# A fused Fourier and two-layer kernel: the second w_out chunk converted in halves, stage A of the second batch entry begun three ticks earlier

## The chip, the cores and the metric

The kernel runs on one core of one Trainium2 chip. The metric is the device time of one execution in microseconds (us). The engines are named as the profile names them: PE (TensorE, matmuls), DVE (VectorE), ACT (ScalarE), POOL (GpSimd) and SP (SyncE, which issues most transfers). Each engine works through its own list of instructions in order and waits on semaphores for the others.

## The reference

```python
def _attn_ref(x) -> np.ndarray:            # x: (2, 3008, 256)
    X = np.fft.fft(x, axis=1)
    X = np.fft.fft(X, axis=2)
    return X.real.astype(np.float32)

def _moe_ref(x, w_in, w_out) -> np.ndarray:     # 6016 tokens, 256 -> 2048 -> 256
    h = x @ w_in
    alpha = 1.0
    g = np.where(h > 0.0, h, alpha * (np.exp(np.minimum(h, 0.0)) - 1.0))
    return (g @ w_out).astype(np.float32)

def _moe2_ref(x, w_in, w_out, alpha) -> np.ndarray:
    h = x @ w_in
    g = np.maximum(h, 0.0) + alpha * np.minimum(h, 0.0)
    return (g @ w_out).astype(np.float32)

def reference(**kwargs):
    ...
    x = attn_out.reshape(B * S, D)
    x = _moe_ref(x=x, **moe_kwargs)
    return _moe2_ref(x=x, **moe2_kwargs)
```

## The kernel before

The real part of the two-dimensional Fourier transform is taken in stages. Stage A is a transform of length 47, four chunks for each of the two batch entries, each chunk in two halves; a half is two PSUM tiles on PE (`stage_a`, L182) that ACT copies to `uc` (L184). When a chunk is whole, SP stores it to DRAM in three pieces (`store_u`) and later loads it back in another order (`load_v`). Stage B (L280, L281) is a transform of length 64; its result is kept as two parts, `hi` by ACT (L290) and `lo`, the remainder, by DVE (L365). The transform along the 256 features is multiplied into the first `w_in`, chunk by chunk (`w_fold`, L376).

All matrix products of the two layers are made of three passes over such pairs (`hi` with `hi`, `lo` with `hi`, `hi` with `lo`). Weights arrive as 64-bit words and are converted first: one ACT instruction (`conv_y`, L333) and three DVE steps (`conv_s`: step 0 at L351, step 1 at L353, step 2 at L355). A split (`w_split`, `hi_lo`) then makes `hi` on ACT (L430) and `lo` on POOL (L431).

The first layer runs in ticks. Tick t takes one block of tokens and 128 of the 2048 hidden columns. Ticks 0 to 7 take block 0 with columns 0 to 7 (in units of 128), ticks 8 to 15 block 1 with the same columns, and so on; four columns make a weight chunk. A tick holds:

- hooks that were put at `pre`
- gemm1(t): six matmuls into two PSUM tiles (L472)
- DVE: `pt` (L605, which reads `zb`) and two `ht` (L609)
- ACT: `hi` of tick t-2 (L584); then the hooks at `mid`; then relu (L625) and exp (L631) of tick t
- POOL: `lo` of tick t-2 (L590); DVE: the combine of tick t-1 (`et`, L577)
- hooks at `end`
- gemm2(t-3): twelve matmuls (L488). Its first matmul needs the `hi` part of the `w_out` half of its columns, its second the `lo` part. In tick 4 it is gemm2(1), in tick 7 gemm2(4), the first to read chunk 1 of `w_out`.

In tick 10, where gemm2(7) ends a group, DVE and ACT also copy the sums out (`xs`, L508, L506) ahead of the combine.

PSUM tiles for gemm1, stage A, stage B, delta and fold come from two pairs of banks, `mm` and `ee`, taken in turn by a counter: whoever adds or moves a tile changes the bank of all later ones.

The order is fixed by tables of tick numbers. `CONV1` has for each weight chunk the tick of the ACT instruction, the ticks of the three DVE steps (at `end`) and the ticks of the two splits; `STAGE_A1` has for each chunk of the second batch entry the tick and place of its halves. `FOLD` puts the fold of `w_in` chunk 2 at the start of tick 11. Delta (L230) is a small product at the start of tick 4, whose result ACT copies to `dt` (L233); stage B of block 1 stands at the start of tick 5.

Of the kernel before, what the change touches and what calls it, by code (L numbers as in the profile page):

```python
# [43 lines left out]
E_PSUM = 42  # L44


CONV1 = [
    (('o', 1, 1), 3, (4, 5, 6), (6, 7)),
    (('i', 1, 2), 7, (7, 8, 9), ()),
    (('i', 1, 3), 10, (10, 12, 13), ()),  # L50
    (('o', 1, 2), 14, (14, 15, 16), (17, 18)),
    (('o', 1, 3), 18, (18, 20, 21), (21, 22)),
]

STAGE_A1 = [
    (0, (7, 'pre'), (8, 'pre')), (1, (9, 'pre'), (11, 'pre')), (2, (12, 'pre'), (14, 'pre')), (3, (16, 'pre'), (17, 'pre')),
]
LOAD_X = {3: 9}
FOLD = {2: (11, 'pre', 0), 3: (15, 'pre', 0)}
# [40 lines left out]
def tile_fft_moe_elu_moe_prelu(  # L100
# [664 lines left out]
    def at(t, fn, *a, where="pre"):  # L765
        hooks[where].setdefault(t, []).append(lambda: fn(*a))
# [4 lines left out]
    def at_conv(t, ts, kind, layer, c, i=None):  # L771

        at(t, conv_y, kind, layer, c, i, where="mid")
        for step in range(3):
            at(ts[step], conv_s, kind, layer, c, i, step, where="end")

    def at_split(t, kind, layer, c, i):
        at(t, w_split, kind, layer, c, i, where="end")
# [7 lines left out]
    with tc.manual_schedule():  # L786
# [27 lines left out]
        }  # L814
        for what, *args in START:
            start[what](*args)
        at_conv(1, (1, 3, 3), "o", 1, 0, 1)
        at_split(3, "o", 1, 0, 1)
        for key, t, ts, splits in CONV1:
            at_conv(t, ts, *key)  # L820
            for i, t_split in enumerate(splits):
# [159 lines left out]
```

## Time and profile before

| what | value |
|---|---|
| device time, median of 3 runs | 962.52 us |
| lowest and highest | 962.43 and 964.06 us |
| device time of the profiled execution | 963.83 us |
| its span, first to last instruction | 961.6 us |
| mean granted TensorE clock | 0.998 |
| busy: PE, DVE, ACT, POOL | 947.0, 715.8, 654.4, 622.7 us |

The profile is of one execution, which took 963.83 us; 2.2 us of that lie outside its span. All places in the text are us from the start of that span. A busy PE says that matmuls were under way, not that the engine was at its peak.

### The profile page before, as it was taken

Reading aid. Unit: us, or ns where it says so; the run is one execution under the profiler, and the core shown is the slowest. Engines: PE = TensorE matmul, PEld = TensorE weight load, DVE = VectorE, ACT = ScalarE, POOL = GpSimd, SP = SyncE. Lnnn points to the kernel's source line nnn. Section 1 sums busy time; section 2 is a strip of 40 time slices with the busy share of each in tenths; the row PEclk is TensorE's granted clock in tenths of the full one; section 3 lists DMA queues with packets and bytes.
Section 4 is the critical chain, followed back from the end, with each engine's and each line's share of the span. In section 5 each row is a group of like instructions: output and inputs, shape, how many; then the busy total and the mean of one; then the engine's idle time right before and its main releaser. Section 6 shows DMA issues by size and latency. Waiting matters only on the chain.

```text
span 961.6 us, 12199 instructions
## 1 busy us (share of the span) xinstructions
PE 947.0 (98%) x4206; PEld 769.3 (80%) x4206; DVE 715.8 (74%) x1012; ACT 654.4 (68%) x914; POOL 622.7 (65%) x495
## 2 busy tenths in 40 slices
PE   8889999999999999999999999999999999999998
PEld 3666778789888878888888888889988888888886
DVE  2896899988999999887777666565657557566564
ACT  5677777766888888888766665565665556565553
POOL 1264577764968779987878855656565664664543
PEclk9999999999999999999999999999999999999999
DMA  8973322201222311121140110020010011001001
GB/s 325 321 228 79 96 77 89 99 25 65 78 75 81 136 44 34 45 88 44 44 154 1 39 45 0 1 88 1 1 56 28 0 45 44 1 1 45 0 1 44
DMA packets 27189, 64.10 MB, mean 67 GB/s; under 512 B 3124, under 2 KB 11572, under 8 KB 25080
## 3 DMA queue, kind: packets, MB, share of 16 engines
q1 hardware_dynamic: 25696, 62.09, 19.3%
q10 hardware_dynamic: 1176, 1.07, 0.3%
q8 instruction: 33, 0.54, 0.2%
q0 software_dynamic: 256, 0.17, 0.1%
q14 instruction: 28, 0.23, 0.1%
HBM read 41.53 MB, written 21.79 MB: 66 GB/s over the span
## 4 chain that ended last, share of the span: by engine, by line
PE 88%; DVE 5%; DMA 3%; ACT 1%; issue 1%; SPq 0%; POOL 0%; ACTq 0%; DVEq 0%
PE acc L488 50%; PE eet L667 13%; PE mmt L667 10%; PE mmt L472 9%; PE eet L472 2%; DMA w<-w_in 1%; DVE et L577 1%; DVE ht L609 1%; DVE pt L605 1%; PE mmt L182 1%; DMA nd<-dt 1%; PE eet L376 1%; PE mmt L281 1%; DMA xc<-x 1%; PE mmt L280 1%
## 5 line engine op out<-in xcount | busy, mean ns | idle before, releaser
L488 PE MATMUL acc<-hi,wo 128*128 128x512 f32 (+1 forms) x1536 | 430.5, 387 | 4.2 <-ACT wo L430 1.5
L693 POOL TENSOR_TENSOR lo<-et,hi 128x512 fp32r<-128x512 f32 (+1 forms) x190 | 237.6, 1281 | 181.0 <-ACT hi L687 181.0
L590 POOL TENSOR_TENSOR lo<-et,hi 128x512 fp32r<-128x512 f32 (+1 forms) x192 | 272.1, 1440 | 107.2 <-ACT hi L584 61.1
L488 PEld LDWEIGHTS acc<-hi,wo 128*128 128x128 f32 x1536 | 288.7, 188 | 61.1 <-ACT wo L430 2.0
L488 PE MATMUL acc<-lo,wo 128*128 128x512 f32 (+1 forms) x768 | 258.3, 387 | 1.3 <-POOL lo L590 1.1
L687 ACT ACTIVATE hi<-et 128x1024 fp32r<-128x1024 f32 (+1 forms) x96 | 100.3, 1045 | 132.5 <-PE acc L488 70.2
L488 PEld LDWEIGHTS acc<-lo,wo 128*128 128x128 f32 x768 | 144.1, 188 | 30.6 <-POOL lo L590 3.4
L625 ACT ACTIVATE et<-ht 128x1024 f32<-128x1024 f32 (+2 forms) x97 | 100.3, 1034 | 68.4 <-DVE ht L609 67.2
L719 DVE TENSOR_TENSOR v<-mmt,p 128x512 f32<-128x512 f32 (+1 forms) x48 | 32.7, 681 | 143.0 <-ACT p L714 143.0
L472 PE MATMUL mmt<-zt,wi 128*128 128x512 f32 (+1 forms) x444 | 116.5, 394 | 1.4 <-DVE ht L609 0.8
L584 ACT ACTIVATE hi<-et 128x1024 fp32r<-128x1024 f32 (+2 forms) x97 | 99.3, 1024 | 5.4 <-DVE et L577 3.9
L609 DVE TENSOR_TENSOR ht<-pt,mmt 128x512 f32<-128x512 f32 (+1 forms) x150 | 95.0, 674 | 8.4 <-PE acc L488 0.5
L472 PEld LDWEIGHTS mmt<-zt,wi 128*128 128x128 f32 x444 | 82.5, 188 | 23.1 <-DVE ht L609 3.4
L744 ACT ACTIVATE et<-mmt 128x512 f32<-128x512 f32 (+1 forms) x96 | 55.8, 590 | 28.8 <-PE mmt L667 14.7
L605 DVE SCALAR_TENSOR_TENSOR pt<-zb,an_sb,mmt 128x512 f32<-128x512 f32 (+1 forms) x73 | 53.4, 731 | 24.7 <-PE mmt L472 24.6
L577 DVE SCALAR_TENSOR_TENSOR et<-et,ht 128x1024 f32<-128x1024 f32 (+2 forms) x44 | 67.3, 1530 | 1.3 <-POOL lo L590 1.1
L574 DVE SCALAR_TENSOR_TENSOR et<-eet,ht 128x512 f32<-128x512 f32 (+1 forms) x106 | 67.1, 674 | 0.0
L747 DVE SCALAR_TENSOR_TENSOR et<-et,oma_sb,eet 128x512 f32<-128x512 f32 (+1 forms) x96 | 66.1, 730 | 0.0
L747 DVE SCALAR_TENSOR_TENSOR et<-et,oma_sb,mmt 128x512 f32<-128x512 f32 (+1 forms) x96 | 66.0, 728 | 0.0
L636 ACT ACTIVATE eet<-et 128x512 f32<-128x512 f32 (+1 forms) x106 | 58.9, 588 | 3.7 <-DVE et L574 2.1
L667 PE MATMUL eet<-xo,wi 128*128 128x512 f32 (+1 forms) x216 | 59.8, 385 | 0.0
L667 PE MATMUL mmt<-xo,wi 128*128 128x512 f32 (+1 forms) x216 | 59.8, 385 | 0.0
(123 smaller groups left out, 1241.6 us busy)
## 6 DMA issues: line engine op xcount, KB each, us to landing
w<-w_in SPq DMA_DIRECT2D x8, 1024.0 KB, 13.5
w<-w_out SPq DMA_DIRECT2D x7, 1024.0 KB, 8.9
ud<-uc SPq DMA_DIRECT2D x20, 256.0 KB, 4.1
vt<-ud SPq DMA_DIRECT2D x5, 1024.0 KB, 4.8
xd<-xs SPq DMA_DIRECT2D x10, 512.0 KB, 3.5
xs<-xd SPq DMA_DIRECT2D x5, 1024.0 KB, 4.8
out_t<-ot SPq DMA_DIRECT2D x16, 256.0 KB, 2.1
xc<-x SPq DMA_DIRECT2D x5, 768.0 KB
```

Of the source, the lines that this page charges most:

```text
L472: mm(out=p[:, 0:n], lhsT=lhsT, rhs=rhs, start=(i == 0), stop=(i == len(ops) - 1))
L488: mm(out=accs[L, bl][d][t][:, 0:n], lhsT=w[:, a, o, d * 128:(d + 1) * 128], rhs=(hi, lo)[b][:, t, 0:n], start=(f == first and i == 0), sto ...
L574: stt(out=s["e"][:, i, :], in0=s["x"][i], scalar=-1.0, in1=s["h"][:, i, :], op0=ALU.add, op1=ALU.max)
L577: stt(out=s["e"][:, i], in0=s["e"][:, i], scalar=-1.0, in1=s["h"][:, i], op0=ALU.add, op1=ALU.max)
L584: act(out=s["hi"][:, i, 0:s["n"]], in_=s["e"][:, i], func=ACTF.Copy)
L590: nc.gpsimd.tensor_tensor(out=s["lo"][:, i, 0:n], in0=s["e"][:, i, :], in1=s["hi"][:, i, 0:n].bitcast(F32), op=ALU.subtract)
L609: tt(out=ht[:, i, 0:n], in0=pt[:, 0:n], in1=p[1], op=op)
L625: act(out=s["e"][:, i], in_=s["h"][:, i], func=ACTF.Relu, scale=-1.0)
L667: mm(out=bank[:, 0:n], lhsT=w[:, a], rhs=x2[b][:, 0:n], start=(first and m == 0), stop=(last and m == 2), skip_group_check=True)
L687: act(out=s["hi"][f][:, :, 0:n], in_=s["g"][f], func=ACTF.Copy)
L693: eng.tensor_tensor(out=s["lo"][f][:, t, 0:n], in0=s["g"][f][:, t], in1=s["hi"][f][:, t, 0:n].bitcast(F32), op=ALU.subtract)
L747: stt(out=o, in0=o, scalar=oma_sb[:, 2 * j + f:2 * j + f + 1], in1=h, op0=ALU.mult, op1=ALU.add)
```

## The change

The list `HALVES` converts the two halves of chunk 1 of the first `w_out` one after the other, each with instructions of half the size: the first half's steps at the ends of ticks 4, 5 and 5, split in tick 6; the second's at the ends of ticks 6, 7 and 7, split in tick 8. Before, the whole chunk's steps stood in ticks 4, 5 and 6 and the splits in ticks 6 and 7. The last step and the split of the second half of chunk 0 move from tick 3 to tick 4. The conversion of `w_in` chunk 2 moves from ticks 7, 7, 8 and 9 to ticks 8, 8, 9 and 10. In stage A of the second batch entry, the first four halves move from ticks 7, 8, 9 and 11 to ticks 4 (at `mid`, behind gemm1), 6, 8 and 9.

```diff
+HALVES = [
+    (('o', 1, 0), 1, 1, (1, 3, 4), 4),
+    (('o', 1, 1), 0, 3, (4, 5, 5), 6),
+    (('o', 1, 1), 1, 5, (6, 7, 7), 8),
+]
 CONV1 = [
-    (('o', 1, 1), 3, (4, 5, 6), (6, 7)),
-    (('i', 1, 2), 7, (7, 8, 9), ()),
+    (('i', 1, 2), 8, (8, 9, 10), ()),
     (('i', 1, 3), 10, (10, 12, 13), ()),
...
 STAGE_A1 = [
-    (0, (7, 'pre'), (8, 'pre')), (1, (9, 'pre'), (11, 'pre')), (2, (12, 'pre'), (14, 'pre')), (3, (16, 'pre'), (17, 'pre')),
+    (0, (4, 'mid'), (6, 'pre')), (1, (8, 'pre'), (9, 'pre')), (2, (12, 'pre'), (14, 'pre')), (3, (16, 'pre'), (17, 'pre')),
 ]
...
-        at_conv(1, (1, 3, 3), "o", 1, 0, 1)
-        at_split(3, "o", 1, 0, 1)
+        for key, i, t, ts, t_split in HALVES:
+            at_conv(t, ts, *key, i)
+            at_split(t_split, *key, i)
```

PE in tick 4, before: delta, gemm1(4), then gemm2(1), whose last matmul is followed by stage B. (`acc` are the sums of gemm2, `r_sb` and `f_sb` the constants of stage B with delta and of stage A.)

```order
L230 MATMUL mmt<-r_sb,vt 8x64
L231 MATMUL mmt<-r_sb,vt 8x64
L472 MATMUL eet<-zt,wi_233 128x512 x6
L488 MATMUL acc_378<-hi,wo_290 128x512 x2
...
L488 MATMUL acc_381<-lo,wo_290 128x512
L280 MATMUL mmt<-r_sb,vt 128x2x64
```

The same place on PE after the change, where all lines of code are four further down.

```order
L234 MATMUL mmt<-r_sb,vt 8x64
L235 MATMUL mmt<-r_sb,vt 8x64
L476 MATMUL eet<-zt,wi_233 128x512 x6
L186 MATMUL mmt<-xc,f_sb 96x512 x2
L492 MATMUL acc_378<-hi,wo_290 128x512 x2
...
L492 MATMUL acc_381<-lo,wo_290 128x512
L284 MATMUL eet<-r_sb,vt 128x2x64
```

Two tiles of stage A stand between gemm1(4) and gemm2(1), in the `mm` banks, one of which delta has just written; stage B moves to the `ee` banks.

ACT from the middle of tick 3, before (`w_408` is chunk 1 of `w_out`, `wo_290` the split chunk 0):

```order
L333 ACTIVATE w_408<-w_252 128x1024
L625 ACTIVATE et<-ht 128x1024
L631 ACTIVATE et<-et 128x1024
L430 ACTIVATE wo_290<-w_270 128x512
L233 ACTIVATE dt<-mmt 8x64
L234 DMA nd_88<-dt 8x64
L584 ACTIVATE hi<-et 128x1024
L625 ACTIVATE et<-ht 128x1024
```

And after:

```order
L337 ACTIVATE w_408<-w_252 128x512
L629 ACTIVATE et<-ht 128x1024
L635 ACTIVATE et<-et 128x1024
L237 ACTIVATE dt<-mmt 8x64
L238 DMA nd_88<-dt 8x64
L588 ACTIVATE hi<-et 128x1024
L188 ACTIVATE uc<-mmt 96x512 x2
L629 ACTIVATE et<-ht 128x1024
```

The conversion has half its size, the split of chunk 0 no longer stands ahead of `dt`, and stage A's two copies stand behind `hi`.

DVE from the end of tick 8 to the end of tick 10, before (`w_301` is the raw `w_in` chunk 2, `w_582` its converted form, which the fold at the start of tick 11 reads):

```order
L353 SCALAR_TENSOR_TENSOR w_301<-w_301 128x1024
L605 SCALAR_TENSOR_TENSOR pt<-zb,an_sb,mmt 128x512
L609 TENSOR_TENSOR ht<-pt,mmt 128x512 x2
L577 SCALAR_TENSOR_TENSOR et<-et,ht 128x1024
L355 SCALAR_TENSOR_TENSOR w_582<-w_582,w_301 128x1024
L605 SCALAR_TENSOR_TENSOR pt<-zb,an_sb,eet 128x512
L609 TENSOR_TENSOR ht<-pt,eet 128x512 x2
L508 COPY xs<-acc_378 128x512
L508 COPY xs<-acc_380 128x512
L577 SCALAR_TENSOR_TENSOR et<-et,ht 128x1024
```

And after, from the end of tick 9 (`w_636` is the converted form now) to the end of tick 10:

```order
L357 SCALAR_TENSOR_TENSOR w_301<-w_301 128x1024
L609 SCALAR_TENSOR_TENSOR pt<-zb,an_sb,mmt 128x512
L613 TENSOR_TENSOR ht<-pt,mmt 128x512 x2
L512 COPY xs<-acc_378 128x512
L512 COPY xs<-acc_380 128x512
L581 SCALAR_TENSOR_TENSOR et<-et,ht 128x1024
L359 SCALAR_TENSOR_TENSOR w_636<-w_636,w_301 128x1024
```

The last step of the conversion has moved from in front of tick 10's `pt` to behind tick 10's combine.

## Rows read from the trace of the kernel before

**Rows 1.** The page's first part: each engine's busy time, share and instructions.

```profile
PE 947.0 (98%) x4206; PEld 769.3 (80%) x4206; DVE 715.8 (74%) x1012; ACT 654.4 (68%) x914; POOL 622.7 (65%) x495
```

**Rows 2.** PE's waits, 32 to 75 us: us in total, times, longest.

```profile
PE acc L488 <- ACT wo L430: 1.5, 1, 1.5
...
PE acc L488 <- POOL wo L431: 0.9, 1, 0.9
PE acc L488 <- POOL lo L590: 0.8, 1, 0.8
```

**Rows 3.** Stretches: length; busy us of PE, PEld, DVE, ACT, POOL; clock; DMA share; GB/s.

```profile
38.00:39.00 1.00, 0.00 (x0) 0.00 (x0) 1.00 (x3) 1.00 (x2) 0.00 (x0) 1.00 0.99 389
70.00:71.00 1.00, 1.00 (x4) 0.73 (x3) 0.51 (x2) 1.00 (x2) 1.00 (x1) 0.50 0.00 0
75.00:145.00 70.00, 70.00 (x273) 50.32 (x271) 61.46 (x66) 53.45 (x67) 41.81 (x28) 1.00 0.34 87
```

**Rows 4.** The chain that ended last: start us, us, what.

```profile
69.20 4.37 PE acc L488 x11
73.57 1.72 PE eet L182 x4
...
76.65 2.72 PE acc L488 x12
...
91.00 3.43 PE eet L376 x8
```

**Rows 5.** Timeline of PE, ticks 4 and 5: start us, us, instruction.

```profile
46.67 2.01 PE L488 MATMUL acc<-hi,wo 128*128 128x512 f32 x8
...
50.47 0.38 PE L280 MATMUL mmt<-r_sb,vt 128*128 128x128 f32 x2
...
53.96 1.62 PE L472 MATMUL eet<-zt,wi 128*128 128x512 f32 x6
```

**Rows 6.** Timeline of DVE, ticks 3 to 10.

```profile
45.92 1.28 DVE L609 TENSOR_TENSOR ht<-pt,mmt 128x512 f32<-128x512 f32 x2
...
50.44 0.69 DVE L355 SCALAR_TENSOR_TENSOR w<-w,w 128x512 int32<-128x512 int32 x1
...
65.91 1.21 DVE L355 SCALAR_TENSOR_TENSOR w<-w,w 128x1024 int32<-128x1024 int32 x1
...
79.30 2.29 DVE L353 SCALAR_TENSOR_TENSOR w<-w 128x1024 int32<-128x1024 int32 x1
...
87.33 0.73 DVE L605 SCALAR_TENSOR_TENSOR pt<-zb,an_sb,eet 128x512 f32<-128x512 f32 x1
88.17 1.28 DVE L609 TENSOR_TENSOR ht<-pt,eet 128x512 f32<-128x512 f32 x2
...
90.58 1.21 DVE L577 SCALAR_TENSOR_TENSOR et<-et,ht 128x1024 f32<-128x1024 f32 x1
91.71 0.70 DVE L351 TENSOR_SCALAR w<-w 128x1024 int32<-128x1024 int32 x1
```

**Rows 7.** Timeline of ACT, ticks 1 to 3.

```profile
39.85 0.66 ACT L333 ACTIVATE w<-w 128x512 f32<-128x512 f32 x1
...
47.11 1.14 ACT L333 ACTIVATE w<-w 128x1024 f32<-128x1024 f32 x1
48.15 1.04 ACT L625 ACTIVATE et<-ht 128x1024 f32<-128x1024 f32 x1
49.23 1.06 ACT L631 ACTIVATE et<-et 128x1024 f32<-128x1024 f32 x1
```

**Rows 8.** SP's own waits, 20 to 75 us.

```profile
SPq L320 <- DMA xc<-x: 1.4, 1, 1.4
```

**Rows 9.** Timeline of SP's issues.

```profile
46.40 0.39 SPq L320 DMA_DIRECT2D w<-w_out  x1
```

**Rows 10.** Timeline of POOL, ticks 7 and 8.

```profile
67.86 1.28 POOL L431 TENSOR_TENSOR wo<-w,wo 128x512 fp32r<-128x512 f32 x1 [2.96 <-ACT wo L430]
...
77.00 3.51 POOL L590 TENSOR_TENSOR lo<-et,hi 128x512 fp32r<-128x512 f32 x2 [2.35 <-ACT hi L584]
```

## The prediction

> **What bounds the kernel now.** I read the engines' totals first: PE is busy 947.0 us, 98% of the span [rows 1]. All that can be saved without removing matmuls is some 15 us, and this change touches ticks 3 to 11 alone. So I went to PE's waits in that stretch [rows 2]: 1.5 us for the ACT half and 0.9 for the POOL half of the `w_out` chunk 1, both in tick 7, and 0.8 us for `lo` in tick 4. The table of stretches shows what follows the wait of tick 7 [rows 3]: at 70 us the granted clock is 0.50 (1.2 GHz). PE idle from 38 to 39 us left it at 1.00 (2.4 GHz). From 75 to 145 us PE is busy for all of 70.00 us at full clock: PE sets the pace there, so what PE has lost or won by then reaches the end undiminished.
>
> The chain gives PE's prices [rows 4]: a half of stage A 1.72 us, gemm2's 12 matmuls 2.72, hence gemm1 76.65 - 73.57 - 1.72 = 1.36; a tick 4.08, with half a stage A 5.80; a fold of `w_in` 3.43. The 11 matmuls after the wait of tick 7 took 4.37 where 11/12 of 2.72 is 2.49: the half clock cost 1.88. From 46.67, where gemm2(1) begins [rows 5], to 73.57, the end of tick 7, are 26.90 us. The work in it is gemm2(1) 2.72, stage B 3.49 (50.47 to 53.96), three ticks 12.24, one half of stage A 1.72: 20.17. So 6.73 us are waits and half clock, and those are what the change can win.
>
> **Step 1, tick 4.** Half of stage A now stands on PE ahead of gemm2(1). Its two tiles need PSUM banks. The first is the bank that `ht`(3) reads until 45.92 + 1.28 = 47.20 [rows 6]. The second is delta's, emptied by ACT's `dt`, which stands behind relu(3) and exp(3). Before, a conversion of 1.14 us at 47.11 precedes these; half of it costs 0.66 [rows 7], so exp(3) ends at 49.23 + 1.06 - 0.48 = 49.8, and `dt`, a short one of 8 rows, near 50.0. PE: first tile 47.2 to 48.1, second 50.0 to 50.9, idle 0.5 + 1.9 = 2.4 us. gemm2(1) runs 50.9 to 53.6 without its wait for `lo`, which was over before 50.47. Stage B ends at 57.1 (before: 53.96). The input `xc` is no cost: SP's wait for it [rows 8] ended when the next load went out at 46.40 [rows 9], 0.8 us before the first tile; later than that, each us is a us.
>
> **Step 2, ticks 5 and 6.** gemm1(5) and gemm2(2) end at 57.1 + 4.08 = 61.2. The second half of chunk 0 is converted a tick later: `pt`(4) takes its place at 50.4, and `pt` (0.84 to the next), `ht` (1.2), the combine (1.2) and the step (0.69) are out at 54.4 alone [rows 6] and about a us later if POOL holds them up; ACT's 0.66 and POOL's 1.28 [rows 10] make it 57.4 at most, needed at 58.7: hidden, with 1 us to spare. The second half of stage A takes stage B's banks, free once DVE has done `pt`, `ht` and two `zt`, which are of `ht`'s size (57.8 + 0.84 + 2 x 1.2 = 61.0): no wait, to 62.9. gemm1(6) and gemm2(3) end at 67.0. The new order on SP puts three stores of stage A ahead of `zb`'s load; they go out once ACT has emptied those banks, near 63.8, and `zb` is read at 75: some 9 us for it, hidden; what it takes beyond them PE would wait.
>
> **Step 3, tick 7.** gemm1(7) ends at 68.3. DVE: `zt` to 61.0, a combine 1.2, two half steps at 0.69: `pt`(6) at 63.7, `ht`(6) ends 0.84 + 1.28 later, 65.8. The first half of chunk 1 is split on ACT behind relu(6) and exp(6) (2.14) [rows 7]: 68.1, + 0.66 = 68.7; POOL's part to 70.1. PE waits 0.4, does one matmul, waits 1.2, and ends the tick at 70.1 + 2.49 = 72.6 at full clock. That is 1.0 us before the old 73.57, with 1.72 us more of work done: **2.7 us won** so far.
>
> **Step 4, ticks 8 to 11.** Ticks 8 and 9 carry half a stage A each, tick 10 none: 72.6 + 2 x 5.80 + 4.08 = 88.3, where PE comes to fold 2 (before: 91.00) [rows 4]. The second half of chunk 1 is split at the end of tick 8, just in time for gemm2(6) at 81.6. But the `w_in` chunk 2 is now converted in ticks 8, 9 and 10 instead of 7, 8 and 9. Its last step stands on DVE at the end of tick 10, behind `pt`(10), `ht`, two copies and the combine; before it stood ahead of `pt`(10). And on PE the half of stage A that lay between gemm2(7) and the fold is gone. From `pt`(10) at 87.33 to the end of the combine at 91.71 are 4.38 us; the step adds 1.21 when alone: 5.6 [rows 6]. `pt`(10) can't begin before the first product of tick 10, 84.2 + 0.7 = 84.9, so PE waits at least 84.9 + 5.6 - 88.3 = 2.2. DVE is later than that: `pt`(9) begins at 80.9, and `pt`, `ht` and the combine (0.84 + 1.2 + 1.2) take it to 84.1. Then comes the middle step, 1.21 alone or 2.29, as at 79.30, when POOL's subtractions run (77.00 for 3.51) [rows 10]. So `pt`(10) begins at 85.3 or 86.4, the fold at 90.9 or 92.0. I take 92.0, because POOL subtracts at the end of tick 9 as at the end of tick 8: a wait of 3.7. The fold ends at 95.4, before at 94.43: **the 2.7 won have become 1.0 lost.**
>
> The Trainium skill, in SBUF — State Buffer, Who interferes with whom, says that a VectorE instruction with two SBUF inputs and a GpSimd one share a port pair as an exclusive lock, for the whole instruction. By that rule the middle step lasts 2.29; the trace agrees (2.29 at 79.30, while POOL subtracts). Without it a gain of 0.1 would stand for the loss of 1.0.
>
> **Step 5, the clock.** Before, PE waited 1.5 and 0.9 us in tick 7 with one matmul between [rows 2], and lost 1.88 us to half clock behind it. The new wait is 3.7 us in one piece, so I charge it the same 1.9: **2.9 us lost in all.** The bounds of this term are 0 and about 1.9 for each of the three waits (2.4, 1.6, 3.7).
>
> From tick 11 on, work and order on PE are the same. DVE's three and ACT's one added instructions (2 x 0.69 for 1.21, 2 x 0.66 for 1.14: 0.2 us each at most) lie beside PE's work or are in the steps above. Sum: the profiled execution's 963.83 (span 961.6 and 2.2 around it) + 2.9 = 966.7. That execution is 1.3 us above the median of 962.52, so I forecast **965.4**.
>
> **Rivals.** A difference of 0.2%, 1.9 us, is what a measurement of this kernel can tell from none: 960.6 to 964.4 is "same".
>
> *The fold's wait is hidden (faster).* Place: PE at tick 11. If DVE gives the last step within 0.8 us of 88.3, the 2.7 us stay won: 959.8 with no wait at all. That is the point that decides. For it: the halves give DVE shorter steps (0.69 for 1.21) ahead of tick 8. Against: even a DVE that is never late needs 5.6 us from `pt`(10), and PE has 3.4 left of tick 10. Chance 0.06.
>
> *The clock does not fall (same).* The wait is 2.2 to 3.7 us and costs only itself: -0.5 to +1.0, 962.0 to 963.5. For it: the idle us at 38 left the clock alone. Against: that is a single us. Chance 0.25.
>
> *The clock falls twice (slower still).* The 2.4 us of tick 4, or the 1.6 of tick 7, bring 1.2 GHz as well: + 4.8, 967.3. For it: the wait of tick 4 is as long in sum as that of tick 7 before [rows 2]. Against: it has 0.86 us of matmuls in its middle, where that had one matmul. Chance 0.24. Here too belongs that chunk 1's split does not come earlier after all and tick 7 keeps its wait and its fall: about as much.
>
> *The forecast*, one fall at the fold: 0.45, 964.4 to 966.4.
>
> **How the numbers follow.** Slower is the forecast and the double fall, 0.69; same 0.25; faster 0.06. The range reaches into the clock that stays (not its lowest end) and over the double fall: 962.4 to 967.8. Outside it are the hidden wait and the tails of the others.
>
> **What would show it.** Step 1: PE waits about 1.9 us for ACT `dt` between two stage A matmuls, near 48 to 50 us. Step 3: PE's waits for the `w_out` split shrink to some 1.6 us and tick 7 ends near 72.6, with clock 1.00 at 70. Step 4: PE waits 2.2 to 3.7 us for DVE's last conversion step ahead of the fold, near 88 to 92. Step 5: a granted clock of 0.50 for some us behind it. The forecast is wrong if the fold's wait is under 1 us, or if the clock falls elsewhere or not at all.

## The result and the profile after

The changed kernel takes 977.18 us (median of 4, 975.33 to 977.49), the kernel before 963.29 in the same comparison (median of 4, 962.43 to 965.20): ratio 1.0138, 95% interval 1.0121 to 1.0156. It is slower, as forecast, but by 13.9 us and not by 2.9. The profiled execution took 977.49 us, its span 975.3.

The page's first part, of the kernel after, beside [rows 1]:

```profile
PE 952.8 (98%) x4206; PEld 771.8 (79%) x4206; DVE 716.3 (73%) x1015; ACT 655.2 (67%) x915; POOL 623.2 (64%) x495
```

PE has the same 4206 instructions and 5.8 us more of busy time: part of the loss is matmuls that ran slower. The rest, 13.7 - 5.8 = 7.9 us of span, is idle time. All lines of code are four further down than before: L492 is gemm2, L434 and L435 the split on ACT and POOL, L359 the last conversion step, L380 the fold. PE's waits (us in total, times, longest), which answer to [rows 2]:

```profile
PE acc L492 <- ACT wo L434: 5.3, 1, 5.3
PE eet L380 <- DVE w L359: 4.3, 2, 3.9
PE mmt L186 <- ACT dt L237: 1.6, 1, 1.6
...
PE acc L492 <- POOL wo L435: 0.6, 1, 0.6
```

The wait for the ACT half of `w_out` chunk 1, 1.5 us before, is 5.3 now. The fold's wait of 3.9 and the 1.6 for `dt` are new, as forecast. The chain that ended last (start us, us, what), ticks 4 to 11, beside [rows 4]:

```profile
50.47 0.20 ACT dt L237
...
51.94 4.24 PE acc L492 x12
...
59.76 0.71 PE mmt L476 x3
...
75.68 0.63 ACT wo L434
...
77.29 0.38 POOL wo L435
...
77.71 4.90 PE acc L492 x11
82.61 1.72 PE mmt L186 x4
...
101.01 1.15 DVE w L359
...
102.20 5.40 PE eet L380 x8
107.60 1.39 PE mmt L476 x6
```

Three groups of matmuls are longer than their like at full clock: gemm2(1) in tick 4 (4.24 for 2.72), gemm2(4) in tick 7 (4.90 for 2.49) and the fold (5.40 for 3.43). The table of stretches has the granted clock behind the busy times, as [rows 3]:

```profile
53.00:56.00 3.00, 3.00 (x10) 2.39 (x9) 3.00 (x3) 2.15 (x3) 2.72 (x2) 0.67 0.96 289
77.00:79.00 2.00, 1.44 (x4) 1.10 (x4) 0.00 (x0) 1.97 (x3) 2.00 (x3) 0.50 0.00 0
104.00:106.00 2.00, 2.00 (x3) 0.68 (x2) 0.00 (x0) 0.49 (x1) 0.00 (x0) 0.50 0.00 0
107.00:177.00 70.00, 69.69 (x302) 53.01 (x301) 63.21 (x69) 51.99 (x65) 45.75 (x31) 1.00 0.24 67
```

The clock is 0.50 (1.2 GHz) behind the waits of tick 7 and of the fold, and 0.67 on the mean in tick 4. From 107 us on it is 1.00, and PE is busy for 69.69 of 70 us. There the chain stands at 107.60, before at 94.43 [rows 4]: 13.2 of the 13.7 us are lost by then.

Why does ACT's split start at 75.68? ACT's timeline in tick 7 (in brackets: idle time before, and what ended it):

```profile
69.67 1.06 ACT L635 ACTIVATE et<-et 128x1024 f32<-128x1024 f32 x1
75.68 0.63 ACT L434 ACTIVATE wo<-w 128x512 fp32r<-128x512 f32 x1 [4.94 <-DVE w L359]
```

And DVE's, ticks 5 to 7:

```profile
65.75 0.69 DVE L359 SCALAR_TENSOR_TENSOR w<-w,w 128x512 int32<-128x512 int32 x1
...
69.62 1.52 DVE L355 TENSOR_SCALAR w<-w 128x512 int32<-128x512 int32 x1
...
74.95 0.69 DVE L359 SCALAR_TENSOR_TENSOR w<-w,w 128x512 int32<-128x512 int32 x1
```

The first half's last step is done at 65.75 + 0.69 = 66.44. ACT is free for the split at 70.7, and yet stands idle for 4.94 us, until the last step of the **second** half (74.95 + 0.69 = 75.64).

### The profile page after: what moved, and what is told of

It reads as the page before. It is cut to its first block, busy times and chain, and to the rows that moved or that the text cites. A ratio compares the mean times of both kernels' runs of the same rounds, so it can differ in the third digit from the quotient of the medians.

```text
span 975.3 us, 12205 instructions
## 1 busy us (share of the span) xinstructions
PE 952.8 (98%) x4206; PEld 771.8 (79%) x4206; DVE 716.3 (73%) x1015; ACT 655.2 (67%) x915; POOL 623.2 (64%) x495
## 4 chain that ended last, share of the span: by engine, by line
PE 85%; DVE 8%; issue 1%; ACT 1%; POOL 0%; DVEq 0%; POOLq 0%; ACTq 0%
PE acc L492 48%; PE eet L671 13%; PE mmt L671 10%; PE mmt L476 8%; DVE et L581 2%; PE eet L476 2%; DVE ht L613 2%; DVE pt L609 1%; PE mmt L186 1%; DVE w L357 1%; PE eet L380 1%; DVE w L359 1%; PE mmt L285 0%; PE eet L285 0%; PE eet L284 0%
## 5 line engine op out<-in xcount | busy, mean ns | idle before, releaser
L492 PE MATMUL acc<-hi,wo 128*128 128x512 f32 (+1 forms) x1536 | 433.0, 389 | 7.7 <-ACT wo L434 5.3
L492 PEld LDWEIGHTS acc<-hi,wo 128*128 128x128 f32 x1536 | 290.0, 189 | 65.6 <-ACT wo L434 5.7
L492 PE MATMUL acc<-lo,wo 128*128 128x512 f32 (+1 forms) x768 | 258.7, 387 | 0.7 <-POOL lo L594 0.5
L492 PEld LDWEIGHTS acc<-lo,wo 128*128 128x128 f32 x768 | 144.5, 189 | 30.0 <-POOL lo L594 2.6
L476 PE MATMUL mmt<-zt,wi 128*128 128x512 f32 (+1 forms) x438 | 114.2, 392 | 0.9 <-DVE ht L613 0.8
```

The lines of the kernel that those rows point to most:

```text
L476: mm(out=p[:, 0:n], lhsT=lhsT, rhs=rhs, start=(i == 0), stop=(i == len(ops) - 1))
L492: mm(out=accs[L, bl][d][t][:, 0:n], lhsT=w[:, a, o, d * 128:(d + 1) * 128], rhs=(hi, lo)[b][:, t, 0:n], start=(f == first and i == 0), sto ...
```

## The experiments

Two theories were tried. **B (buffer):** in the code, the raw words of `w_out` chunk c and its split are tiles of one name in one pool:

```python
        home, tag = (big, "big") if (kind, layer, c) in wd else (wp, f"w{kind}{c}")
...
        nm = f"w{kind}{c}"
...
            ws[layer, c] = wp.tile(shape, F32R, tag=nm, name=nm)
```

The split of chunk 1 is written where its raw words lay, so its first half has to wait until both halves of the raw words have been read. By the shapes in the code, what ACT writes in tick 6 (the first quarter of the tile) covers raw words of the first half only, which were read by 66.44: under B the wait is not for those bytes but for the old tile as a whole. **C (converted tile):** both halves stand in one converted tile (`w_408`), and its reader is released only with that tile's last write.

Chunk 0 was split by halves before the change too. Its raw words have another name (`wo3`), so it can't show B, but its halves share one converted tile (`w_270`), and the kernel before split the first of them on ACT 16 us ahead of the second one's last step, which stood at 50.44 [rows 6]:

```profile
34.62 0.64 ACT L430 ACTIVATE wo<-w 128x512 fp32r<-128x512 f32 x1 [1.03 <-DVE w L355]
```

That speaks against C already.

All results, in us; ratios are to the kernel before, run on the same chip, whose medians there were 963.65 to 964.05:

| run | median | ratio | 95% interval |
|---|---|---|---|
| e1, chunk 1's raw words in a buffer of their own | 968.90 | 1.0050 | 1.0037 to 1.0063 |
| e2, `w_in` chunk 2 back in ticks 7 to 9 | 970.04 | 1.0066 | 1.0052 to 1.0079 |
| e5, both | 963.82 | 1.0003 | 0.9995 to 1.0012 |
| e11, second half's steps a tick earlier | 973.44 | 1.0090 | 1.0075 to 1.0104 |
| e3, before + earlier stage A | 967.65 | 1.0042 | 1.0029 to 1.0055 |
| e4, before + halves | 969.54 | 1.0061 | 1.0048 to 1.0075 |
| e8, before + later `w_in` chunk 2 | 968.04 | 1.0046 | 1.0034 to 1.0059 |
| e10, e4 + buffer of its own | 964.26 | 1.0013 | 1.0004 to 1.0022 |
| e6, before + stage A in 5, 6, 7, 9 | 965.18 | 1.0017 | 1.0008 to 1.0026 |
| e7, before + stage A in 6, 7, 8, 9 | 960.97 | 0.9973 | 0.9963 to 0.9983 |
| e9, e5 with e7's stage A | 961.48 | 0.9979 | 0.9970 to 0.9988 |

**e1: a buffer of its own** (the changed kernel, and):

```diff
-     ('load', 'i', 1, 2), ('load', 'x', 1, 1), ('load', 'o', 1, 2), ('load', 'x', 1, 2), ...
+     ('load', 'i', 1, 2), ('load', 'x', 1, 1), ('load', 'x', 1, 2), ...
-... else (wp, f"w{kind}{c}")
+... else (wp, "wo2" if (kind, layer, c) == ("o", 1, 1) else f"w{kind}{c}")
+        at(9, load, ("o", 1, 2))
```

> The changed kernel with the raw words of chunk 1 of w_out loaded into a buffer other than the one that its split halves are written to (raw chunk 2 is loaded later, in tick 9, to make room). The changed kernel's PE waited 5.3 and 0.6 us in tick 7 for the first split half of chunk 1. Theory B (buffer): the split's output tile takes the place of the raw words, so ACT has to wait until DVE has read the last of them (the second half's last step, done at 75.64), though the first half's own steps were done at 66.44. Then the wait for the ACT half goes, what is left in tick 7 is 0 to 1.5 us for POOL's half, the half clock behind it (2.4 us) goes or shrinks, and the time is 977.2 - 5 to 8 = 969 to 972. Theory C (converted tile): ACT waits since both halves stand in one converted tile and its reads are only released with that tile's last write. That tile is as before here, so the 5.3 us stay and the time is 976 to 978. The fold's wait (3.9 us, 2.0 us of half clock) stays in either.

Its time is 968.90, 8.3 us less and just under the range for B. PE's waits, then the split on ACT, the second half's last step on DVE, and gemm2(4) in the chain:

```profile
PE eet L380 <- DVE w L359: 4.2, 2, 3.8
...
PE acc L492 <- POOL wo L435: 0.9, 1, 0.9
```

```profile
69.86 0.61 ACT L434 ACTIVATE wo<-w 128x512 fp32r<-128x512 f32 x1
```

```profile
75.88 0.69 DVE L359 SCALAR_TENSOR_TENSOR w<-w,w 128x512 int32<-128x512 int32 x1
```

```profile
71.89 2.77 PE acc L492 x11
```

The split now starts 6 us ahead of that step and PE waits 0.3 us for it. The converted tile is shared as before, so C falls and B stands.

**e11: the same buffer, read to its end earlier** (the changed kernel, and):

```diff
-    (('o', 1, 1), 1, 5, (6, 7, 7), 8),
+    (('o', 1, 1), 1, 5, (6, 6, 6), 8),
```

> The changed kernel with one number changed: DVE's second and third step of chunk 1's second half stand at the end of tick 6, not of tick 7. Raw words and split share their buffer as in the changed kernel, the first half's conversion is where it was. Theory B (the first half's split waits for the last read of the raw words): in the changed kernel that read ended at 75.64; moved behind the first step (69.62, 1.52 us) it ends near 72.5, so the split and PE come 3.1 us earlier: the wait of 5.3 us falls to 2 to 2.5, and the time by 3 (with the same half clock behind the wait) to 5.5 us (without it): 971.5 to 974.5. If the wait had nothing to do with the second half's steps it would stay at 5.3 us, or grow by the 1.4 us of steps that now stand ahead of pt of tick 7: 977 or above. The fold's wait stays at 3.5 to 4 us in either.

973.44, inside B's range. PE's waits, then the chain:

```profile
PE eet L380 <- DVE w L359: 3.8, 1, 3.8
PE acc L492 <- ACT wo L434: 2.2, 1, 2.2
```

```profile
69.89 0.70 DVE w L359
70.59 0.02 issue
70.61 0.63 ACT wo L434
```

The split follows the second half's last step at 0.02 us, wherever that step stands: the wait of 5.3 us is 2.2. No load and no buffer differs from the changed kernel here, as they do in e1. Taken alone e11 doesn't tell B from C, since the same step reads the raw words last and writes the converted tile last; e1 and chunk 0 do.

**e2: `w_in` chunk 2 as before** (the changed kernel, and):

```diff
-    (('i', 1, 2), 8, (8, 9, 10), ()),
+    (('i', 1, 2), 7, (7, 8, 9), ()),
```

> The changed kernel with w_in chunk 2 converted in ticks 7, 8 and 9 again, as before. The changed kernel's PE waited 3.9 us for the last of these steps ahead of fold 2, and the fold took 5.40 us instead of 3.43. If that wait comes from the later tick of the steps, both go: 977.2 - 5.9 = about 971, with 5.3 us of wait in tick 7 unchanged or longer (the first w_in step now stands on DVE in tick 7 too). Rival: DVE is late anyway, from the second half of chunk 1 that is converted in ticks 6 and 7, and the fold still waits over 2 us: 975 to 977.

970.04: the fold has no wait and takes 3.43 us again; tick 7 waits 5.3 us as in the changed kernel. PE's longest wait, and the fold in the chain:

```profile
PE acc L492 <- ACT wo L434: 5.3, 1, 5.3
```

```profile
96.34 3.43 PE eet L380 x8
```

**e5: e1 and e2 together.**

> The changed kernel with both repairs at once: raw chunk 1 in a buffer of its own, and w_in chunk 2 converted in ticks 7, 8 and 9 again. What stays of the change are the halves and the earlier stage A. Theory B, with the two waits independent: the repairs alone took 977.2 to 968.9 and to 970.0, that is 8.3 and 7.2 us; together 15.5, so 961 to 963, beside 964 for the kernel before: the gain that the halves were counted on for (2.7 us, less a wait of 1.6 us in tick 4 and its half clock) is there. Rival: the one wait had covered work of the other (the first w_in step now stands in tick 7, beside the second half's steps), so the sum is not reached: 965 or above.

963.82, no different from the kernel before. No wait came back: PE's are 0.3 and 0.9 us in tick 7, none at the fold, and 0.4 and 1.6 in tick 4. The sum of the two repairs (15.4 us) is missed by 2.0, and the median lies in neither of the two ranges. The profiled execution, at 962.11 and a mean clock of 1.0, lies within the first (961 to 963); the others, at 963.5 to 964.4 and 0.996 to 0.998, don't. So what is missing is of the size of one more fall of the clock, but where that falls was not seen.

**e3, e4, e8: each part alone on the kernel before.** e3 has the new row of `STAGE_A1`; e8 the new row of `w_in` chunk 2; e4 the list `HALVES` and the loop over it in place of chunk 1's old row.

> The kernel before with only the earlier stage A (ticks 4, 6, 8, 9); both w_out chunk 1 and w_in chunk 2 are converted as before. Theory B: no raw words are read late here, so tick 7's wait is that of before or a little less (1.5 to 3 us) and not 6; the fold doesn't wait; but the wait of tick 4 for ACT's dt is longer, since the whole chunk's conversion (1.14 us) stands ahead of it: 3.5 to 4 us with half clock behind it. Time 965 to 968. If instead the earlier stage A by itself makes tick 7 wait 5 us or more, it isn't the halves: 970 or above.

967.65, within its range. PE waits 3.6 us for `dt`, 1.6 and 0.9 in tick 7, nothing at the fold. In the chain, gemm2(1) follows the wait of 3.6 at half clock, and gemm2(4) the waits of 1.6 and 0.9 at full:

```profile
54.37 4.80 PE acc L488 x12
...
76.94 2.76 PE acc L488 x11
```

> The kernel before with only the conversion of chunk 1 in halves; stage A and w_in chunk 2 stand where they did. Theory B: PE does not come to tick 7 later than before, but the first half's split still waits for the second half's last step, so PE waits 5 to 6 us there, with half clock behind it: 970 to 973, slower by itself. Theory C says the same here (the two are told apart by the run with a buffer of its own). Rival: the long wait only appears because stage A is moved ahead (PE is later or earlier there): then tick 7 waits under 2.5 us and the time is 961 to 964.

969.54, just under the range. PE waits 5.2 us for the split in tick 7 with stage A and `w_in` unmoved: the long wait is the halves' own. Another 0.6 and 0.9 us of wait stand in tick 5, of which e10 tells more.

> The kernel before with only the conversion of w_in chunk 2 a tick later (8, 9 and 10). The prediction's step 4 on its own: the last step stands on DVE at the end of tick 10, behind pt, ht, two copies and the combine, and PE comes to fold 2 at about 91: a wait of 2 to 2.5 us, which is shorter than the changed kernel's 3.9 since PE does half a stage A more between; with half clock behind the wait 967 to 969, without it 965.5 to 967. Rival: the step is late only since the halves and stage A push DVE; then no wait and 963 to 965.

968.04, within its range. The fold waits 2.0 us, and its row in the chain shows the half clock:

```profile
93.14 5.40 PE eet L376 x8
```

By ratio the three parts cost 0.42, 0.61 and 0.46%, 1.49 in sum; the whole change cost 1.38. Each part loses by itself.

**e10: e4 with a buffer of its own.**

> The run with the halves alone (969.5, stage A and w_in as in the kernel before) with one thing more: the raw words of chunk 1 in a buffer of their own. Theory B: of its 5.2 us of wait for the ACT half at most 1.5 stay, and its half clock (1.8 us) goes or stays as in the kernel before: 961 to 964.5, so the halves then cost nothing against 963.7 or gain up to 2.5. Rival: the halves cost by themselves (more instructions on DVE and ACT, later raw chunk 2), the wait is not the buffer's alone: 966 or above.

964.26, 0.13% above the kernel before and within the range for B. The wait of 5.2 has become 1.3 us, with 0.9 for POOL's part behind it. The other two waits for a split stand in tick 5, ahead of gemm2(2):

```profile
56.48 0.50 PE L492 MATMUL acc<-hi,wo 128*128 128x512 f32 x1 [0.64 <-ACT wo L434]
57.83 1.88 PE L492 MATMUL acc<-hi,wo 128*128 128x512 f32 x7 [0.85 <-POOL wo L435]
...
69.13 0.50 PE L492 MATMUL acc<-hi,wo 128*128 128x512 f32 x1 [1.32 <-ACT wo L434]
70.49 1.87 PE L492 MATMUL acc<-hi,wo 128*128 128x512 f32 x7 [0.86 <-POOL wo L435]
```

The wait in tick 5 is for the second half of chunk 0, whose last step and split the first row of `HALVES` has moved from tick 3 to tick 4. The kernel before has no wait there, and the changed kernel has none because its PE comes 3 us later. So the halves of chunk 1 leave 2.2 us of wait in tick 7, where the kernel before has 2.4, and the moved split costs 1.5 us. No run has the halves of chunk 1 without that first row, so what they would bring by themselves stays open.

**e6 and e7: other places for stage A**, the conversions as before.

```diff
-    (0, (7, 'pre'), (8, 'pre')), (1, (9, 'pre'), (11, 'pre')), ...
+    (0, (5, 'mid'), (6, 'pre')), (1, (7, 'pre'), (9, 'pre')), ...
...
-    (0, (7, 'pre'), (8, 'pre')), (1, (9, 'pre'), (11, 'pre')), ...
+    (0, (6, 'pre'), (7, 'pre')), (1, (8, 'pre'), (9, 'pre')), ...
```

> The kernel before with stage A of the second batch entry's first tiles in ticks 5, 6, 7 and 9 instead of 7, 8, 9 and 11; all conversions as before. Theory: what stage A's halves do for PE is to fill ticks in which it would wait; tick 4 has no bank and no dt ready for them, ticks 5 and 6 have. Then no wait for dt, tick 7's wait for the split stays at 1 to 2 us or goes, and the time is 959 to 962. Rival: tick 5 has its stall too (the bank that stage B or the product of delta holds), and the 2 to 4 us stand there instead: 964 to 967.

965.18, the rival's range. PE's timeline, and DVE's:

```profile
59.17 3.11 PE L182 MATMUL mmt<-xc,f_sb 96*96 96x512 f32 x4 [3.19 <-issue]
```

```profile
58.38 1.28 DVE L365 TENSOR_TENSOR zt<-mmt,zt 128x512 fp32r<-128x512 f32 x2
```

Stage A waits 3.19 us in tick 5, takes 3.11 us for the usual 1.72, and starts as the first of the two `zt`, which read stage B's `mm` banks, is done (58.38 + 0.6 to 0.7). The profile names no releaser; that it is this bank is argued from the times.

> The kernel before with stage A's halves in ticks 6, 7, 8 and 9 instead of 7, 8, 9 and 11; all conversions as before. PE gets half a stage A (1.7 us) ahead of the wait of tick 7 (1.5 and 0.9 us, and 1.9 us of half clock behind it): if that wait is set by DVE's conversion alone it shrinks to 0.5 to 1 us and the half clock goes: 960 to 962. Rival: the conversion is put back by the work of the earlier half, and the wait stays: 963 to 965.

960.97: with two pairs of numbers changed it beats both kernels, by 0.27% the one before and by some 1.7% the changed one. The chain:

```profile
69.77 2.80 PE acc L488 x11
...
88.30 3.43 PE eet L376 x8
```

In tick 7 only POOL's 0.9 us of wait is left, gemm2(4) runs at full clock, and the fold begins at 88.30 instead of 91.00 [rows 4].

**e9: e7's stage A, with the halves, the buffer and the old `w_in` row of e5.**

> All that the runs so far speak for in one kernel: chunk 1 of w_out in halves with raw words in a buffer of their own, w_in chunk 2 in ticks 7, 8 and 9, stage A's halves in ticks 6, 7, 8 and 9. Theory B, with the bank theory for tick 4: no wait for dt in tick 4, none for the ACT half in tick 7, and the fold does not wait. The same places of stage A with the whole chunk converted at once gave 960.97 with 0.9 us of wait for POOL's half left in tick 7. If that half comes earlier by the shorter conversion, 959.5 to 961; if the halves give nothing beside the earlier stage A (POOL's part is set by its own 1.3 us behind relu and exp of tick 6), 960.5 to 962, the same as without them.

961.48, in the range for halves that give nothing. Its interval and e7's overlap. But PE's waits for a split are not those of e7:

```profile
56.25 0.50 PE L492 MATMUL acc<-hi,wo 128*128 128x512 f32 x1 [0.62 <-ACT wo L434]
57.60 1.90 PE L492 MATMUL acc<-hi,wo 128*128 128x512 f32 x7 [0.85 <-POOL wo L435]
...
81.51 1.88 PE L492 MATMUL acc<-hi,wo 128*128 128x512 f32 x7 [0.28 <-POOL wo L435]
```

None is left in tick 7, where e7 waits 0.9 us, and 0.3 stand in tick 9 for the second half; but 0.6 and 0.9 stand in tick 5 for chunk 0's moved split. So the nothing is a sum: what the halves of chunk 1 win in tick 7, less what the list's first row costs in tick 5.

## Why the prediction was right in direction and wrong in size

The direction came out for a reason that was given, the fold (Steps 4 and 5), and for one that was not: ticks 4 to 7, which were to win 2.7 us, lost 7.3. With the wait of Step 3 mended (e1) the change costs 4.9 us, not 13.9, against the forecast's 2.9.

The account of the profiled executions, forecast 966.7 against 977.49, from the chain's rows: stage B ends at 59.76, not 57.1 (+2.7); tick 7 ends 82.61 - 59.76 = 22.85 us later, not 72.6 - 57.1 = 15.5 (+7.3, all of it in tick 7); ticks 8 to 10 take 102.20 - 3.87 - 82.61 = 15.7, as forecast (3.87 is the fold's longest wait); the fold with its wait takes 9.3 instead of 3.7 + 3.43 + 1.9 = 9.0 (+0.2); from 107.60 to the end are 867.7 us, before 867.2 (+0.5). The sum is 10.7 of the 10.8.

**Step 1, tick 4: right but for the clock.** PE waits 0.4 and 1.6 us for the two banks (forecast 0.5 and 1.9), and not for `lo`. The second tile began at 50.72, not 50.0: 0.7 of the 2.7 us. `dt` began at 50.47; in e2 and e11, whose kernels differ from this one only from tick 6 on, at 49.91 and 50.12, so 0.4 to 0.6 of the 0.7 are spread between executions. gemm2(1) lost 1.5 us to half clock, which the sum had at nothing; 0.5 are the slower tile of stage A and the start of stage B.

**Step 2: right.** gemm1(7) ends 71.07 - 59.76 = 11.3 us behind stage B, forecast 11.2; PE has no wait in ticks 5 and 6. The 71.07 come from the first row of gemm2(4) on PE's timeline, 76.36 less its idle time:

```profile
76.36 0.80 PE L492 MATMUL acc<-hi,wo 128*128 128x512 f32 x1 [5.29 <-ACT wo L434]
```

**Step 3 failed: "The first half of chunk 1 is split on ACT behind relu(6) and exp(6): 68.1".** The step let the split depend on its own half's conversion and on ACT's order alone. It asked what the split reads and not where it writes. e1 takes the shared buffer away and the wait goes; e11 moves the last read and the wait goes with it. PE came to the second matmul of gemm2(4) 77.71 - 71.07 = 6.6 us behind gemm1(7), not 1.8: 4.8 us. The eleven matmuls then took 4.90, for 2.49 in the sum; at full clock they take 2.77 (e1's chain), so 2.1 are a fall of the clock and 0.3 were sized too small. At the end of tick 7 PE stands 9.0 us behind the kernel before [rows 4] with 1.72 us more done: "2.7 us won" were 7.3 lost. The rival that came nearest ("chunk 1's split does not come earlier after all and tick 7 keeps its wait") had the place but kept the old wait. In fact the split came later: before, the whole chunk's last step stood at 65.91 [rows 6], in tick 6; the second half's stands in tick 7.

**Step 4: right.** The wait of the fold was 3.9 us for 3.7, for the step that was named, and e8 shows it alone. The middle step lasted 2.25 us, for 2.29 [rows 6]. In the chain, and in POOL's timeline:

```profile
94.39 2.25 DVE w L357
```

```profile
92.01 3.54 POOL L594 TENSOR_TENSOR lo<-et,hi 128x512 fp32r<-128x512 f32 x2 [0.66 <-POOL wo L435]
```

POOL's two subtractions end at 92.01 + 3.54 = 95.55; 1.21 us behind that are 96.76, and the step ended at 94.39 + 2.25 = 96.64. The Trainium skill (SBUF — State Buffer, Who interferes with whom) calls the port pair that the two engines share an exclusive lock for a whole instruction; by that rule the step does nothing until POOL is done, and the trace agrees to 0.1 us. No run here took POOL's work away, but before, at 61.03, a middle step of the same size took 1.21 us while POOL stood idle (60.03 to 62.39):

```profile
61.03 1.21 DVE L353 SCALAR_TENSOR_TENSOR w<-w 128x1024 int32<-128x1024 int32 x1
```

**Step 5: a term mis-sized.** One fall of 1.9 us was charged and bounds of 1.9 for each of three waits were named. All three waits brought a fall in the profiled execution: 1.5, 2.1 and 2.0 us, 5.6 in all, beside the 5.8 us that PE's busy time grew. Only the fold's had been charged.

So of the 10.7 us, 4.8 are the wait of Step 3, 3.6 are the two falls that were not charged, and the rest small terms (0.7 ahead of stage A, 0.5 in tick 4, 0.3 in gemm2(4), 0.2 at the fold, 0.5 behind it).

## What to carry to other kernels

When work is cut into halves so that the first can be used early, look at what its output overwrites as well as at what it reads: where input and output share a buffer, the first half is as late as the last read of the second. That holds even where the bytes that it overwrites were read long ago, if the buffer is handed over as a whole. Work that fills an engine's waits belongs where its own inputs and banks are free already; of three earlier places tried for stage A the one that won was that with hardly a wait of its own (0.5 us). The cutting into halves, with the moved split of chunk 0 that came with it, added nothing to it. A new wait of 2 us on PE can bring a half clock behind it, here of 1.5 to 2.1 us where it came, and a forecast should charge it.

## What was not expected of the hardware

The length of a wait did not tell whether TensorE's clock falls behind it. In tick 4, with the same waits of 0.4 and 1.6 us, gemm2(1) took 4.24 us in the changed kernel, 3.71 in e1, and 2.73 to 2.75 (full clock) in e2, e5 and e11. In e1 the clock fell a tile earlier: with the second tile of stage A ahead of it, gemm2(1) took 5.46 us in the changed kernel, 5.47 in e1 and 3.83 to 3.85 in the other three, so the fall cost 1.6 in both. In tick 7, waits of 1.5 and 0.9 us were followed by half clock before (4.37 us for eleven matmuls) [rows 4] and in e8 (4.38), and waits of 1.6 and 0.9 in e3 by full clock (2.76). The price of that fall before was therefore 1.6 us, not the 1.88 of the prediction. At the fold, a wait of 2.0 us (e8) cost the same 2.0 as waits of 3.8 and 3.9 did. Executions of one program differ by it, as far as the mean clock tells: of the 21 of the kernel before beside e9 and e10, 8 took 962.2 to 962.7 us at 0.997 to 0.999, and 13 took 963.6 to 966.4 at 0.994 to 0.998, and of the 24 beside e5 to e8, 11 took 962.1 to 963.1 and 13 took 963.6 and more, while e7's eight all lay within 0.7 us, seven of them at 1.0. What decides in which execution the clock falls stays open: each kernel has one trace.
